# Attention and experts on one core: the value products dealt out by credit, their evictions placed anew

## The chip, the cores and the metric

The kernel runs on one core of a Trainium2 chip. The metric is device time in microseconds (us) of one execution. The five engines run side by side, each in the order of its own program, and wait for one another through semaphores: TensorE (PE, with its weight loads shown apart as PEld), VectorE (DVE), ScalarE (ACT), GpSimd (POOL) and SyncE (SP), which here issues most of the DMAs.

## The reference

Two stages. The first is attention over 8 batches of 8 heads, 576 positions, 64 channels, in which scores that lie more than tau below their row's maximum are dropped:

```python
scores = scale * np.matmul(q, k.transpose(0, 1, 3, 2))
thresh = np.max(scores, axis=-1, keepdims=True) - tau
scores = np.where(scores >= thresh, scores, -1000000000.0)
...
attn = np.exp(scores)
attn = attn / (np.sum(attn, axis=-1, keepdims=True) + 1e-09)
return np.matmul(attn, v).astype(np.float32)
```

The second gives each of the 4608 resulting rows of 512 to one of 8 experts, at most 576 rows each, in order of falling gate logits, and puts the rows through that expert's two matrices:

```python
logits = x @ w_gate
...
for e in range(E):
    mask = assigned == e
    h = np.maximum(x[mask] @ w1[e], 0.0)
    out[mask] = h @ w2[e]
```

## The kernel before

**Tiles and slots.** Two heads make a pair; four pairs make a batch, 32 pairs in all. The scores of a pair are cut into 9 tiles of 128 rows by 576 keys (the ninth holds the last 64 rows of both heads). The attention runs in slots of two tiles, 4.5 slots to a pair and 18 to a batch. The loop `for s_ in range(-2,NT//2+2)` (line 261) writes each engine's program slot by slot; slot numbers here are the values of `s_`. What stands earlier there stands earlier in the engine's queue. In slot s the tiles go through these steps:

- scores of tiles 2s+4 and 2s+5 by TensorE into `sc` (line 69). There are two such buffers, so the next slot's scores wait until VectorE has read these.
- first pass by VectorE (line 74): scale, row minimum, copy to `z`. This is the head of a slot as the trace is cut here. ScalarE takes the exponential (line 85), GpSimd adds tau to the threshold (line 75).
- second pass by VectorE (line 89), one slot later: drop what is under the threshold, and sum.
- transposes by TensorE into `tb` (line 98), two slots after the scores. There is one such buffer of two tiles, so they wait until ScalarE has evicted the slot before (lines 114, 116) into `pt`.
- in the slot after a pair's ninth tile, the leftover keys (64 of the 576) are transposed as well, ten small transposes ahead of the slot's other work (lines 118 and 122), and evicted into `pl` (lines 121, 127, 128). They use the same buffer `tb`. I call these leftover slots; each pair has one.

**Value products.** For a pair, the product with the values has two halves of 288 rows. Each half needs four units (line 139, two matmuls each, by 128 keys) and a last column (line 145, two matmuls, from the leftover keys), all summed in one bank `xo`. ScalarE evicts each half into `xt` (line 148).

**What orders them.** `queue` holds the units of all pairs that are ready, in order; `aux` holds the work of a finished batch: the swap of reciprocals (line 159), two halves of the gate logits (line 170), their transposes (lines 177 and 187), and for batches 0 and 1 five row units that turn `xt` back into rows (line 199; VectorE scales them in line 206). All of these, and the halves `xo`, share two banks. The parts of a slot that place them:

- `columns` takes 2 units, or 3 where the queue is longer than 10 entries. While a pair is not begun, it lets up to `GAP`=3 pieces of `aux` go first.
- `whole` takes the last columns of both halves at once (`pl_units`), when the pair's units are all done; else, while no pair is open, up to two pieces of `aux`.
- `flush` issues the evictions that the slot before has left over, at the start of the slot, ahead of the transposes' evictions in ScalarE's queue. Both halves of a pair are evicted there together.

A pair's `pt` and `pl` are allocated with its first transposes (line 106), which need the pair two before to be finished.

After the last slot the rows of batches 2 to 7 are made, beside the search for the first expert's rows, and then the experts' stage runs. It depends on the logits of the last batch; its code is the same in both kernels.

Of the kernel before, what the change touches and what calls it, by code (L numbers as in the profile page):

```python
# [16 lines left out]
PSUM = bass.MemoryType.PSUM  # L17
IOA = bass.IndirectOffsetOnAxis
S=576; D=64; HS=288; QK=3*HS+2*S
PPB=8; LTB=1; VTB=5; HOLD=1; GAP=3; NBO=2; XAC=(4,); NDEF=4; XTB=4; XTY=1.05; XT0=2.0; XRB=2  # L20


def attention(ctx, tc, qk, vl, tau, wgd, xrows, xts, Lg, nb_batches, ident, swap, R, after_first):
    nc=tc.nc
# [70 lines left out]
    PT={}; PL={}; TB={}  # L95
# [6 lines left out]
        return TB[k]  # L102
    def tr(t,first):
        p,i=divmod(t,9)
        if p not in PT:
            PT[p]=wk.tile([128,2,4,S],F32,name="pt"); PL[p]=wk.tile([128,S],F32,name="pl")
        tb=bank(t,first)
        pv=pview(t)
        o=64 if (i<8 and i%2) else 0
        for kb in range(4): turn(tb[:,:,kb],pv[:,o+kb*128:o+(kb+1)*128])  # L110
    def trev(t):
        p,i=divmod(t,9); tb=TB.pop(t)
        if i<8:
            A.activation(PT[p][:,i%2,:,(i//2)*128:(i//2+1)*128].rearrange("p k (r q) -> p r k q",r=2),tb,AF.Copy)  # L114
        else:
            A.activation(PT[p][:,:,:,512:576],tb,AF.Copy)
# [13 lines left out]

    have={}
    XT={}; XO={}
    def pv_unit(p,f,u):
        b,j=divmod(p,4)
        if b not in XT: XT[b]=wk.tile([128,4,S],F32,name="xt",bufs=XTB)
        if u==0: XO[p,f]=ps_v.tile([128,512],F32,name="xo")
        xo=XO[p,f]; q=slice(f*HS,(f+1)*HS); v=LD[p]["v"]
        for h in range(2):
            T.matmul(xo[64*h:64*h+64,:HS],v[:,u,64*h:64*h+64],PT[p][:,h,u,q],start=(u==0),stop=False,skip_group_check=True)  # L139
    def pl_units(p):  # L140
        b,j=divmod(p,4)
        for f in range(2):
            q=slice(f*HS,(f+1)*HS); xo=XO[p,f]
            for h in range(2):
                T.matmul(xo[64*h:64*h+64,:HS],LD[p]["v"][:,4,64*h:64*h+64],PL[p][:,q],start=False,stop=True,skip_group_check=True)
# [4 lines left out]

    RD={}
    def rd_calc(b):
        rd=wk.tile([128,4,9],F32,name="rd",bufs=XTB+NBO); RD[b]=rd
        V.tensor_scalar(rd,DEN[b],1e-9,None,op0=ALU.add)
        V.reciprocal(rd,rd)
    def rd_unit(b):
        rd=RD[b]
        ps=ps_v.tile([128,512],F32,name="xo")
        T.matmul(ps[:,:4],swap,rd[:,:,8],start=True,stop=True)
        rm=wk.tile([128,4,2],F32,name="rm",bufs=XTB+NBO); RD["m",b]=rm  # L160
        def ev():
            V.tensor_copy(rm[0:64,:,0],rd[0:64,:,8]); V.tensor_copy(rm[64:128,:,1],rd[64:128,:,8])
            V.tensor_copy(rm[0:64,:,1],ps[0:64,:4]); V.tensor_copy(rm[64:128,:,0],ps[64:128,:4])
        return ev
    LT={}
    def lg_unit(b,f):
        if f==0: LT[b]=wk.tile([128,S+D],F32,name="lt",bufs=LTB)
        ps=ps_v.tile([128,512],F32,name="xo")
        for j in range(4):
            T.matmul(ps[32*j:32*j+32,:HS],wg[:,j],XT[b][:,j,f*HS:(f+1)*HS],start=True,stop=True,tile_position=(0,32*j))  # L170
        def ev():
            A.activation(LT[b][:,f*HS:(f+1)*HS],ps[:,:HS],AF.Copy)
            if f==1: G.tensor_scalar(LT[b][:,S:],LT[b][:,S-D:S],1.0,0.0,op0=ALU.mult,op1=ALU.add)
        return ev
    def lgt_unit(b):
        ps=ps_v.tile([128,4,128],F32,name="xo")
        for c in range(4): T.transpose(ps[:,c],LT[b][:,c*128:(c+1)*128],ident)
        def ev():
            w=wk.tile([128,4,2,4,8],F32,name="lw",bufs=1)
            lv=ps.rearrange("p c (j r) -> p c j r",j=4)  # L180
            for h in range(2):
                V.tensor_tensor(w[:,:,h],lv[:,:,:,8*h:8*h+8],RD[b][:,:,h:8:2].rearrange("p j c -> p c j").unsqueeze(3).to_broadcast([128,4,4,8]),op=ALU.mult)
            V.tensor_reduce(Lg[:,4*b:4*b+4,:],w.rearrange("p c h j e -> p c e (h j)"),axis=AX.X,op=ALU.add)
        return ev
    def lgm_unit(b):
        ps=ps_v.tile([128,4,128],F32,name="xo")
        T.transpose(ps[:,0],LT[b][:,512:640],ident)
        r=slice(64*(b%2),64*(b%2)+64)
        def ev():
            w=wk.tile([128,4,2,8],F32,name="lwm",bufs=1)  # L190
            lv=ps[:,0].rearrange("p (j r) -> p j r",j=4)[:,:,:16].rearrange("p j (h e) -> p j h e",h=2)
            V.tensor_tensor(w[r],lv[r],RD["m",b][r].unsqueeze(3).to_broadcast([64,4,2,8]),op=ALU.mult)
            V.tensor_reduce(Lg[r,32+b//2,:],w[r].rearrange("p j h e -> p e (j h)"),axis=AX.X,op=ALU.add)
        return ev
    def xt_unit(b,c):
        ps=ps_v.tile([128,4,128],F32,name="xo")
        n=128 if c<4 else 64
        for j in range(4):
            T.transpose(ps[:n,j],XT[b][:,j,c*128:c*128+n],ident)
# [18 lines left out]
    def push_pair(p):  # L220
        b,j=divmod(p,4)
        for f in range(2):
            for u in range(4):
                need=(p,"t5" if f==0 else "t8")
                queue.append(("c",lambda need=need: have.get(need,1<<30)+HOLD<=st["slot"],lambda f=f,u=u: pv_unit(p,f,u)))
        if j==3: queue.append(("n",lambda: True,lambda: rd_calc(b)))
        queue.append(("f",lambda: have.get((p,"pl"),1<<30)+HOLD<=st["slot"],lambda: pl_units(p)))
        if (b,j)==(0,0): queue.append(("n",lambda: True,R.consts))
        if (b,j)==(nb_batches-1,2): queue.append(("n",lambda: True,lambda: (R.prep(0,28),R.compare(R.k("E1"),J,0,28))))
        if j==3:  # L230
            queue.append(("n",lambda: True,lambda: aux.extend([(0,lambda: rd_unit(b)),(0,lambda: lg_unit(b,0)),(0,lambda: lg_unit(b,1)),
                (1,lambda: lgt_unit(b)),(0,lambda: lgm_unit(b))])))
            rows=[lambda c=c: xt_unit(b,c) for c in range(5)]
            if nb_batches-NDEF-NBO<=b<nb_batches-NDEF:
                queue.append(("n",lambda: True,lambda: nc.sync.dma_start(xts[b],XT[b])))
                late2.extend(rows)
            elif b<nb_batches-NDEF: queue.append(("n",lambda: True,lambda: aux.extend([(0,x) for x in rows])))
            else: late.extend(rows)
# [3 lines left out]
    def plain():
        while queue and queue[0][0]=="n" and queue[0][1]() and not later: queue.pop(0)[2]()
    def columns(n):
        while n and queue and queue[0][0]=="c" and queue[0][1]():
            if not st["open"] and aux and st["aux"]<GAP and st["slot"]>=st["last"]+aux[0][0]: return
            queue.pop(0)[2](); st["open"]=True; n-=1
    def whole():
        while queue and queue[0][0]=="n" and queue[0][1]() and st["open"]: queue.pop(0)[2]()
        if st["open"]:  # L250
            if queue and queue[0][0]=="f" and queue[0][1]():
                later.append(queue.pop(0)[2]()); st["open"]=False; st["aux"]=0
            return
# [543 lines left out]
```

## Time and profile before

| | us |
|---|---|
| median of 3 runs | 1052.82 (1052.12 to 1054.36) |
| profiled execution, time | 1053.07 |
| profiled execution, span from first to last instruction | 1051.3 |
| head of the first slot (s = -2) | 5.39 |
| head of slot 23 | 86.02 |
| head of slot 59 | 215.50 |
| heads of slots 77, 95 and 113 (three batches on end) | 275.29, 335.34, 395.12 |
| head of the last slot (s = 141) | 489.42 |

A span runs from the first to the last instruction of the execution; the time of the run is a little longer. The attention fills the first half of the span. Shares of busy time over the span (PE 93%, DVE 74%, ACT 61%, POOL 32%) are means over both stages; what a change in the attention is worth is read from windows inside it.

In a time line a row gives the start, the length, the engine, line and operation, what is written and from what, the count, and in brackets the idle time before it and who ended it. Ends of matmuls are modelled; the distance from one start to the next is what a group takes of TensorE's time.

### The profile page before, as it was taken

Reading aid. Unit: us, or ns where it says so; the run is one execution under the profiler, and the core shown is the slowest. Engines: PE = TensorE matmul, PEld = TensorE weight load, DVE = VectorE, ACT = ScalarE, POOL = GpSimd, SP = SyncE. Lnnn points to the kernel's source line nnn. Section 1 sums busy time; section 2 is a strip of 40 time slices with the busy share of each in tenths; the row PEclk is TensorE's granted clock in tenths of the full one; section 3 lists DMA queues with packets and bytes.
Section 4 is the critical chain, followed back from the end, with each engine's and each line's share of the span. In section 5 each row is a group of like instructions: output and inputs, shape, how many; then the busy total and the mean of one; then the engine's idle time right before and its main releaser. Section 6 shows DMA issues by size and latency. Waiting matters only on the chain. (4 is left out here: it accounts for less than half of the span.)

```text
span 1051.3 us, 24035 instructions
## 1 busy us (share of the span) xinstructions
PE 977.3 (93%) x9104; PEld 715.4 (68%) x9104; DVE 777.3 (74%) x2085; ACT 640.4 (61%) x1221; POOL 331.3 (32%) x485
## 2 busy tenths in 40 slices
PE   6899999999999999999767999999999999999996
PEld 3555555555555555555457869889797988889895
DVE  6989988988989899898567767758586677744230
ACT  5888787888888888887454434435353534445340
POOL 2333443433333333333453535420303021132201
PEclk9999999999999999999877999999999999999998
DMA  5212331342422222111455061432424042363101
GB/s 220 105 60 100 119 110 48 131 154 102 150 104 68 92 105 105 55 53 50 163 187 169 12 198 48 149 108 91 156 91 161 17 151 106 103 234 126 51 9 42
DMA packets 35715, 113.03 MB, mean 108 GB/s; under 512 B 4368, under 2 KB 4752, under 8 KB 35088
## 3 DMA queue, kind: packets, MB, share of 16 engines
q1 hardware_dynamic: 28496, 89.47, 23.9%
q0 software_dynamic: 5888, 18.88, 5.7%
q10 hardware_dynamic: 1216, 3.15, 0.9%
q8 instruction: 72, 1.18, 0.5%
q14 instruction: 43, 0.35, 0.1%
HBM read 89.19 MB, written 21.23 MB: 105 GB/s over the span
## 5 line engine op out<-in xcount | busy, mean ns | idle before, releaser
L75 POOL TENSOR_SCALAR nb<-nb,taub 128x1 f32<-128x1 f32 x288 | 158.1, 550 | 302.8 <-DVE z L74 272.3
L74 DVE TENSOR_SCALAR_CACHE_REDUCE z<-sc 128x576 f32<-128x576 f32 x288 | 206.0, 751 | 49.4 <-PE sc L69 48.6
L85 ACT ACTIVATE pp<-z,nb 128x576 f32<-128x576 f32 x256 | 187.3, 772 | 35.9 <-DVE z L74 34.9
L89 DVE SCALAR_TENSOR_TENSOR pp<-z,nb,pp 128x576 f32<-128x576 f32 x256 | 199.9, 813 | 0.3
L664 PE MATMUL pf<-w2h,H 128*128 128x512 f32 x576 | 196.1, 402 | 1.1 <-DVE H L340 1.1
L69 PE MATMUL sc<-qk 64*128 64x288 f32 (+1 forms) x1280 | 183.4, 430 | 7.4 <-DMA qk<-qk_dram 6.1
L139 PE MATMUL xo<-pt,vt 128*64 128x288 f32 x1024 | 147.4, 416 | 4.4 <-DVE xr L206 2.8
L98 PEld LDWEIGHTS tb<-ident,pp 64*128 64x128 f32 x2304 | 85.8, 139 | 90.2 <-ACT pt L114 36.8
L114 ACT ACTIVATE pt<-tb 128x512 f32<-128x512 f32 x256 | 139.7, 592 | 6.7 <-PE tb L98 4.0
L98 PE MATMUL tb<-ident,pp 64*128 64x64 f32 x2304 | 108.8, 230 | 21.6 <-ACT pt L114 14.6
L664 PE MATMUL pf<-w2l,H 128*128 128x512 f32 x320 | 128.2, 401 | 0.0
L671 POOL DMA_INDIRECT out_dram<-y,idx x40 | 41.3, 1033 | 267.9 <-ACT y L667 163.1
L69 PEld LDWEIGHTS sc<-qk 64*128 64x128 f32 (+1 forms) x1280 | 93.3, 179 | 40.4 <-DVE z L74 9.2
L664 PEld LDWEIGHTS pf<-w2h,H 128*128 128x128 f32 x576 | 106.4, 189 | 20.0 <-DVE H L340 1.5
L644 PE MATMUL pf<-xh,w1h 128*128 128x288 f32 x512 | 113.3, 300 | 1.2 <-ACT xh L627 1.2
L644 PE MATMUL pf<-xh,w1l 128*128 128x288 f32 x512 | 113.7, 300 | 0.0
L644 PE MATMUL pf<-xl,w1h 128*128 128x288 f32 x512 | 113.0, 299 | 0.0
L139 PEld LDWEIGHTS xo<-pt,vt 128*64 128x64 f32 x1024 | 64.6, 136 | 67.1 <-issue 27.7
L650 ACT ACTIVATE hf<-pf 128x576 f32<-128x576 f32 x64 | 41.7, 651 | 105.4 <-PE pf L644 92.0
L667 ACT ACTIVATE y<-pf 128x512 f32<-128x512 f32 x40 | 23.9, 597 | 116.0 <-PE pf L664 99.4
L644 PEld LDWEIGHTS pf<-xh,w1h 128*128 128x128 f32 x512 | 82.9, 189 | 3.7 <-ACT xh L627 1.7
L644 PEld LDWEIGHTS pf<-xl,w1h 128*128 128x128 f32 x512 | 82.6, 189 | 0.2 <-DVE xl L340 0.2
(170 smaller groups left out, 1350.0 us busy)
## 6 DMA issues: line engine op xcount, KB each, us to landing
qk<-qk_dram SPq DMA_DIRECT2D x31, 1008.0 KB, 5.5
w2s<-w_dram SPq DMA_DIRECT2D x32, 512.0 KB, 6.0
w1s<-w_dram SPq DMA_DIRECT2D x28, 512.0 KB, 5.6
vt<-vl_dram SPq DMA_DIRECT2D x32, 320.0 KB, 5.8
xrows<-pp SPq DMA_DIRECT2D x24, 256.0 KB, 2.0
xts<-xt SPq DMA_DIRECT2D x2, 1152.0 KB, 5.2
pt<-xts SPq DMA_DIRECT2D x2, 1152.0 KB
xrows<-xr SPq DMA_DIRECT2D x8, 256.0 KB, 2.1
```

The costliest lines, as they stand in the source:

```text
L69: T.matmul(sc[o,f,:HS], kd["q",h][r,c], kd[k,h][r,:],start=True,stop=True)
L74: V.tensor_scalar(z,SC.pop(t)[:,:,:HS],-0.125,None,op0=ALU.mult,op1=ALU.min,accum_out=nb[:,0:1])
L75: G.tensor_scalar(nb[:,1:2],nb[:,0:1],taub[:,0:1],None,op0=ALU.add)
L85: A.activation(pview(t),ZB[t].rearrange("p a b -> p (a b)"),AF.Exp,bias=NBI[t][:,0:1],scale=-1.0)
L89: V.scalar_tensor_tensor(pv,ZB.pop(t).rearrange("p a b -> p (a b)"),NBI[t][:,1:2],pv,op0=ALU.is_le,op1=ALU.mult,accum_out=den_of(p)[:,p%4, ...
L98: g=slice(64*r,64*r+64); T.transpose(o[:,r],x[g],ident[g,g])
L114: A.activation(PT[p][:,i%2,:,(i//2)*128:(i//2+1)*128].rearrange("p k (r q) -> p r k q",r=2),tb,AF.Copy)
L139: T.matmul(xo[64*h:64*h+64,:HS],v[:,u,64*h:64*h+64],PT[p][:,h,u,q],start=(u==0),stop=False,skip_group_check=True)
L644: T.matmul(ps[:,h,:HS],s[w][:,k,f*128:(f+1)*128],s[x][:,k,h*HS:(h+1)*HS], start=(k==0 and j==0),stop=(k==3 and j==2))
L650: A.activation(hf,ps[:,:,:HS],AF.Relu)
L664: T.matmul(ps[:,0,:],H[:,f,c:c+128],s[w][:,f],start=(f==0 and j==0),stop=e)
L671: G.indirect_dma_start(out=out,out_offset=IOA(ap=s["idx"][:n,t:t+1],axis=0),in_=y[:n],in_offset=None)
```

## The change

The units are dealt out by a credit: each slot adds `RATE`=2.4, up to `CAPV`=3.3, and each unit and each half's last column takes 1. The last column follows its own half's four units (`pl_unit`), and each half is evicted when it is done. A half is only begun when the bank of two halves before is free (`free_v`). Work of `aux` is placed only when no half is open, so behind a last column; `columns` stops there for it.

In slots in which the ninth tile is evicted (the leftover slots), `flush` moves behind the transposes' evictions. `pt` and `pl` are allocated at the first eviction instead of the first transposes.

```diff
-PPB=8; LTB=1; VTB=5; HOLD=1; GAP=3; NBO=2; XAC=(4,); NDEF=4; XTB=4; XTY=1.05; XT0=2.0; XRB=2
+PPB=8; LTB=1; VTB=5; HOLD=1; CAPV=3.3; RATE=(2.4,2.4); NBO=2; XAC=(4,); NDEF=4; XTB=4; XTY=1.05; XT0=2.0; XRB=2
...
     def trev(t):
         p,i=divmod(t,9); tb=TB.pop(t)
+        if i==0: PT[p]=wk.tile([128,2,4,S],F32,name="pt"); PL[p]=wk.tile([128,S],F32,name="pl")
...
+    banks=[]; VB={}
+    def bank_v(sh):
+        t=ps_v.tile(sh,F32,name="xo"); banks.append([False]); VB[id(t)]=banks[-1]
+        return t
+    def free_v(): return len(banks)<2 or banks[-2][0]
...
-    def pl_units(p):
+    def pl_unit(p,f):
         b,j=divmod(p,4)
-        for f in range(2):
-            q=slice(f*HS,(f+1)*HS); xo=XO[p,f]
-            for h in range(2):
-                T.matmul(xo[64*h:64*h+64,:HS],LD[p]["v"][:,4,64*h:64*h+64],PL[p][:,q],start=False,stop=True,skip_group_check=True)
-        have[p,"pv"]=1
-        def ev():
-            for f in range(2): A.activation(XT[b][:,j,f*HS:(f+1)*HS],XO.pop((p,f))[:,:HS],AF.Copy)
-        return ev
+        q=slice(f*HS,(f+1)*HS); xo=XO.pop((p,f))
+        for h in range(2):
+            T.matmul(xo[64*h:64*h+64,:HS],LD[p]["v"][:,4,64*h:64*h+64],PL[p][:,q],start=False,stop=True,skip_group_check=True)
+        if f==1: have[p,"pv"]=1
+        return VB[id(xo)],lambda: A.activation(XT[b][:,j,q],xo[:,:HS],AF.Copy)
...
+        for f in range(2):
+            for u in range(4): queue.append(("c",when("t5" if f==0 else "t8"),u==0,lambda f=f,u=u: pv_unit(p,f,u)))
+            if (f,j)==(0,3): queue.append(("n",when("t8"),False,lambda: rd_calc(b)))
+            queue.append(("c",when("pl"),False,lambda f=f: pl_unit(p,f)))
...
+    def columns():
+        while queue and queue[0][1]():
+            if queue[0][0]=="c":
+                if st["credit"]<1 or (queue[0][2] and not free_v()): return
+                st["credit"]-=1
+            c,_,_,g=queue.pop(0); r=g()
+            if c=="c" and r:
+                later.append(r)
+                if aux: return
     def whole():
...
         n=0
-        while n<2 and aux and st["slot"]>=st["last"]+aux[0][0]:
-            r=aux.pop(0)[1](); n+=1; st["aux"]+=1; st["last"]=st["slot"]
+        while n<2 and aux and not XO and free_v() and st["slot"]>=st["last"]+aux[0][0]:
+            r=aux.pop(0)[1](); n+=1; st["last"]=st["slot"]
...
-        flush(); plain()
+
+        if not any(t%9==8 for t in ev_): flush()
         for t in ev_:
-            p,i=divmod(t,9); trev(t); have[p,f"t{i}"]=s_
+            p,i=divmod(t,9)
+            while i==0 and p>1 and (p-2,"pv") not in have: st["credit"]=9; columns(); flush()
+            trev(t); have[p,f"t{i}"]=s_
+        flush()
...
-        columns(3 if len(queue)>10 else 2)
-        if any(t%9==0 and t>=18 for t in tr_):
-            while (max(tr_)//9-2,"pv") not in have: columns(9); whole(); flush(); plain()
-        else: whole()
+        st["credit"]=min(st["credit"]+RATE[bool(aux)],CAPV)
+        columns(); whole()
```

What this does to TensorE's program in a steady batch (slots 95 to 112 in both kernels), beside the scores and the sixteen transposes that every slot has. "Left" is the leftover block, "v" a value unit, "c" one half's last column, "swap" the swap of reciprocals, "g" one half of the logits, "t" their transposes; "(6)" marks the slots with a ninth tile of scores, which have six matmuls for scores in place of four. VectorE's work from the swap, the logits' transposes and the row units stands between a slot's second pass and the next head; the reciprocals (lines 154 and 155) stand in the 17th slot before, in the 15th after.

| slot of the batch | before | after |
|---|---|---|
| 1 | left, swap, g | left, 2v |
| 2 (6) | g | c, swap |
| 3 | 2v | 3v |
| 4 | 3v | v, c, g |
| 5 | left, 3v, 2c | left, 3v |
| 6 | 5t | v, c, g |
| 7 (6) | 2v | 2v |
| 8 | 3v | 2v, c, 4t |
| 9 | 3v, 2c | 2v |
| 10 | left, 2v | left, 2v |
| 11 (6) | 2v | c, 1t |
| 12 | 2v | 3v |
| 13 | 2v, 2c | v, c |
| 14 | left, 3v | left, 3v |
| 15 | 2v | v, c |
| 16 (6) | 2v | 2v |
| 17 | v, 2c | 2v, c |
| 18 | none | 2v |

In slots 23 to 58 the five row units of batches 0 and 1 ("x") are placed too. Before, they stand two, two and one to a slot (slots 29, 32, 33 and 47, 50, 51). After, one to a slot, and the logits of batch 1 move back. These slots then differ from the table:

| slot | after | slot | after |
|---|---|---|---|
| 35 | v, c, x | 48 | 2v, c, g |
| 37 | v, c, x | 51 | c, g |
| 39 | 2v, c, x | 53 | v, c, 4t |
| 42 | c, x | 55 | v, c, 1t |
| 44 | v, c, x | 57 | 2v, c, x |
| 46 | v, c, swap | | |

The other four row units of batch 1 stand in slots 60, 62, 64 and 66.

TensorE's rows at slot 117, the fifth of a batch, and the one behind it. `sc` are scores, `tb` transposes, `xo<-pt,vt` value units (two rows each), `xo<-pl,vt` last columns, `xo<-xt,wg` and `xo<-ident,lt` the logits. Before:

```order
L69 MATMUL sc<-qk 128x288 x4
L98 MATMUL tb<-ident,pp 128x64 x8
L98 MATMUL tb<-ident,pm 128x64 x2
L139 MATMUL xo<-pt,vt 64x288 x6
L145 MATMUL xo<-pl,vt 64x288 x4
L98 MATMUL tb<-ident,pp 128x64 x16
L69 MATMUL sc<-qk 128x288 x4
L177 MATMUL xo<-ident,lt 128x128 x4
L187 MATMUL xo<-ident,lt 128x128
L98 MATMUL tb<-ident,pp 128x64 x16
```

And after:

```order
L69 MATMUL sc<-qk 128x288 x4
L98 MATMUL tb<-ident,pp 128x64 x8
L98 MATMUL tb<-ident,pm 128x64 x2
L144 MATMUL xo<-pt,vt 64x288 x6
L98 MATMUL tb<-ident,pp 128x64 x16
L69 MATMUL sc<-qk 128x288 x4
L144 MATMUL xo<-pt,vt 64x288 x2
L149 MATMUL xo<-pl,vt 64x288 x2
L172 MATMUL xo<-xt,wg 32x288 x4
L98 MATMUL tb<-ident,pp 128x64 x16
```

The four matmuls of the last columns have left the leftover slot; the slot behind it now holds a value unit, one half's last column and half of the logits.

ScalarE's rows at two leftover slots. `pt<-tb` evicts transposes, `xt<-xo` a half of the values' product, `pl<-tb` the leftover keys, `pp<-z,nb` is the exponential. Before (slot 104's kind, the tenth of a batch, with both halves of the slot before in front):

```order
L148 ACTIVATE xt<-xo 128x288 x2
L116 ACTIVATE pt<-tb 128x8x64
L114 ACTIVATE pt<-tb 128x2x4x64
L121 ACTIVATE pl<-tb 128x2x4x64
L127 ACTIVATE pl<-tb 64x64
L128 ACTIVATE pl<-tb 64x64
```

After (slot 108's kind, the fourteenth, which follows a last column):

```order
L113 ACTIVATE pt<-tb 128x2x4x64
L115 ACTIVATE pt<-tb 128x8x64
L151 ACTIVATE xt<-xo 128x288
L120 ACTIVATE pl<-tb 128x2x4x64
L126 ACTIVATE pl<-tb 64x64
L127 ACTIVATE pl<-tb 64x64
```

The eviction of a half now stands behind those of the transposes and ahead of that of the leftover keys, and it is one where there were two.

More of the change, by code (lines that the diff above doesn't have):

```diff
@@ L104, in tr @@
         p,i=divmod(t,9)
-        if p not in PT:
-            PT[p]=wk.tile([128,2,4,S],F32,name="pt"); PL[p]=wk.tile([128,S],F32,name="pl")
         tb=bank(t,first)
@@ L135, in pv_unit @@
         if b not in XT: XT[b]=wk.tile([128,4,S],F32,name="xt",bufs=XTB)
-        if u==0: XO[p,f]=ps_v.tile([128,512],F32,name="xo")
+        if u==0: XO[p,f]=bank_v([128,512])
         xo=XO[p,f]; q=slice(f*HS,(f+1)*HS); v=LD[p]["v"]
@@ L157, in rd_unit @@
         rd=RD[b]
-        ps=ps_v.tile([128,512],F32,name="xo")
+        ps=bank_v([128,512])
         T.matmul(ps[:,:4],swap,rd[:,:,8],start=True,stop=True)
@@ L167, in lg_unit @@
         if f==0: LT[b]=wk.tile([128,S+D],F32,name="lt",bufs=LTB)
-        ps=ps_v.tile([128,512],F32,name="xo")
+        ps=bank_v([128,512])
         for j in range(4):
@@ L175, in lgt_unit @@
     def lgt_unit(b):
-        ps=ps_v.tile([128,4,128],F32,name="xo")
+        ps=bank_v([128,4,128])
         for c in range(4): T.transpose(ps[:,c],LT[b][:,c*128:(c+1)*128],ident)
@@ L185, in lgm_unit @@
     def lgm_unit(b):
-        ps=ps_v.tile([128,4,128],F32,name="xo")
+        ps=bank_v([128,4,128])
         T.transpose(ps[:,0],LT[b][:,512:640],ident)
@@ L195, in xt_unit @@
     def xt_unit(b,c):
-        ps=ps_v.tile([128,4,128],F32,name="xo")
+        ps=bank_v([128,4,128])
         n=128 if c<4 else 64
@@ L214, in xt_unit, with when @@
         return ev
-    queue=[]; aux=[]; later=[]; late=[]; late2=[]; st={"open":False,"aux":0,"last":-9,"slot":0}
+    queue=[]; aux=[]; later=[]; late=[]; late2=[]; st={"last":-9,"slot":0,"credit":0.0}
     def push_pair(p):
         b,j=divmod(p,4)
+        def when(n): return lambda: have.get((p,n),1<<30)+HOLD<=st["slot"]
         for f in range(2):
[L223 to L238, printed above, removed]
@@ new lines, in push_pair @@
+            for u in range(4): queue.append(("c",when("t5" if f==0 else "t8"),u==0,lambda f=f,u=u: pv_unit(p,f,u)))
+            if (f,j)==(0,3): queue.append(("n",when("t8"),False,lambda: rd_calc(b)))
+            queue.append(("c",when("pl"),False,lambda f=f: pl_unit(p,f)))
+        if (b,j)==(0,0): queue.append(("n",lambda: True,False,R.consts))
+        if (b,j)==(nb_batches-1,2): queue.append(("n",lambda: not aux,False,lambda: (R.prep(0,28),R.compare(R.k("E1"),J,0,28))))
+        if j==3: queue.append(("n",lambda: not later,False,lambda: finish(b)))
@@ L239, in flush, with finish @@
+    def finish(b):
+        aux.extend([(0,lambda: rd_unit(b)),(0,lambda: lg_unit(b,0)),(0,lambda: lg_unit(b,1)),(1,lambda: lgt_unit(b)),(0,lambda: lgm_unit(b))])
+        rows=[lambda c=c: xt_unit(b,c) for c in range(5)]
+        if nb_batches-NDEF-NBO<=b<nb_batches-NDEF:
+            nc.sync.dma_start(xts[b],XT[b]); late2.extend(rows)
+        elif b<nb_batches-NDEF: aux.extend([(0,x) for x in rows])
+        else: late.extend(rows)
     def flush():
-        for g in later: g()
+        for k,g in later: g(); k[0]=True
@@ L241, in flush @@
         later.clear()
[L242 to L247, printed above, removed]
-    def whole():
[L249 to L253, printed above, removed]
-        n=0
-        while n<2 and aux and st["slot"]>=st["last"]+aux[0][0]:
-            r=aux.pop(0)[1](); n+=1; st["aux"]+=1; st["last"]=st["slot"]
-            if callable(r): later.append(r)
+    def columns():
[7 more added lines that the diff above has]
+                if aux: return
@@ L258, in attention @@
+    def whole():
+        n=0
+        while n<2 and aux and not XO and free_v() and st["slot"]>=st["last"]+aux[0][0]:
+            r=aux.pop(0)[1](); n+=1; st["last"]=st["slot"]
+            later.append((banks[-1],r))
     load(0);
@@ L286, in attention @@
     while queue or aux or later:
-        st["slot"]+=1; flush(); plain(); columns(9); whole()
+        st["slot"]+=1; st["credit"]=9; flush(); columns(); whole()
     for k in range(0,NBO,2):
```

## The prediction

> **What bounds the kernel now.** I read the page first, for its span, then the list of waits over the attention, then windows cut at batch borders, and last the time lines of VectorE and TensorE inside one batch.
>
> ```profile
> span 1051.3 us, 24035 instructions
> ```
> ```profile
> DVE z L74 <- PE sc L69: 48.6, 43, 3.8
> ```
> The second row is from the waits of the first 530 us. VectorE's first pass (line 74) is the head of every slot, and in 43 slots it stood still for scores, 48.6 us in all.
>
> A slot is two tiles of scores; 18 slots are one batch. These windows run from the head of one slot to the head of a later one (columns: length; busy us and count of PE, PEld, DVE, ACT, POOL; clock; DMA share; GB/s).
>
> ```profile
> 275.29:335.34 60.05, 57.55 (x671) 33.69 (x671) 54.66 (x158) 51.18 (x95) 19.83 (x41) 1.00 0.33 118
> 86.02:215.50 129.48, 120.48 (x1382) 71.80 (x1382) 114.80 (x321) 103.49 (x189) 49.62 (x82) 1.00 0.28 102
> ```
> A steady batch is 60.05 us with VectorE busy for 54.66: at most 5.4 us of a batch can be gained by removing waits alone. The second window is 36 slots in which ten units of row output are made as well.
>
> How short can a slot be? VectorE's time line, two successive heads without a wait, and two with one:
>
> ```profile
> 281.80 0.75 DVE L74 TENSOR_SCALAR_CACHE_REDUCE z<-sc 128x576 f32<-128x576 f32 x1
> 284.64 0.75 DVE L74 TENSOR_SCALAR_CACHE_REDUCE z<-sc 128x576 f32<-128x576 f32 x1
> ...
> 287.52 0.76 DVE L74 TENSOR_SCALAR_CACHE_REDUCE z<-sc 128x576 f32<-128x576 f32 x1
> 292.44 0.76 DVE L74 TENSOR_SCALAR_CACHE_REDUCE z<-sc 128x576 f32<-128x576 f32 x1 [2.00 <-PE sc L69]
> ```
> The first is 2.84 us, VectorE's own pace. The second is 4.92 with 2.00 of waiting. TensorE in that slot and the next:
>
> ```profile
> 286.77 1.19 PE L69 MATMUL sc<-qk 64*128 64x288 f32 x8
> 288.11 0.46 PE L98 MATMUL tb<-ident,pp 64*128 64x64 f32 x8 [0.15 <-ACT pt L116]
> ...
> 288.56 1.68 PE L139 MATMUL xo<-pt,vt 128*64 128x288 f32 x12
> 290.07 1.14 PE L145 MATMUL xo<-pl,vt 128*64 128x288 f32 x8
> 291.14 0.71 PE L98 MATMUL tb<-ident,pp 64*128 64x64 f32 x16
> 291.69 1.19 PE L69 MATMUL sc<-qk 64*128 64x288 f32 x8
> 292.81 0.66 PE L177 MATMUL xo<-ident,lt 128*128 128x128 f32 x4
> 293.30 0.27 PE L187 MATMUL xo<-ident,lt 128*128 128x128 f32 x1
> 293.50 0.71 PE L98 MATMUL tb<-ident,pp 64*128 64x64 f32 x16
> ```
> From start to start: scores 1.12, leftover block 0.45 after a wait of 0.15, twelve value records 1.51, the last columns of both halves 1.07, transposes 0.55. TensorE is simply full here: from scores to scores 4.92. The next slot has almost nothing on it. So the wait comes from **lumps**, and dealing the value units evenly attacks it.
>
> **The change, part by part.** No product is added or removed. The trace counts a value matmul twice and a transpose once, so the prices are: a slot's scores and transposes 1.67; one value unit 1.51/3 = 0.50 (I use 0.51); one half's last column 1.07/2 = 0.535; leftover block 0.60 with its wait; four transposes of logits 0.49, a single one 0.20. The others:
>
> ```profile
> 277.82 1.35 PE L69 MATMUL sc<-qk 64*128 64x288 f32 x12
> 279.10 0.69 PE L170 MATMUL xo<-xt,wg 128*32 128x288 f32 x8
> ...
> 504.07 1.18 PE L170 MATMUL xo<-xt,wg 128*32 128x288 f32 x16 [0.54 <-DVE rm L163]
> 505.28 0.92 PE L177 MATMUL xo<-ident,lt 128*128 128x128 f32 x4
> ...
> 106.66 1.35 PE L199 MATMUL xo<-ident,xt 128*128 128x128 f32 x8 [0.37 <-DVE lw L182]
> 107.94 0.71 PE L98 MATMUL tb<-ident,pp 64*128 64x64 f32 x16
> ```
> Twelve score records take 1.28 (0.16 over eight), one half of the logits 1.21/2 = 0.60, a row unit 1.28/2 = 0.64. VectorE's side work, which lengthens its slot beyond 2.84:
>
> ```profile
> 295.29 0.48 DVE L182 TENSOR_TENSOR lw<-xo,rd 128x128 f32<-128x128 f32 x2
> ...
> 296.45 0.23 DVE L192 TENSOR_TENSOR lwm<-xo,rm 64x64 f32<-64x64 f32 x1
> ...
> 297.01 0.76 DVE L74 TENSOR_SCALAR_CACHE_REDUCE z<-sc 128x576 f32<-128x576 f32 x1
> ```
> ```profile
> L206 DVE TENSOR_TENSOR xr<-xo,rd 128x512 f32<-128x512 f32 x8 | 5.1, 681 | 0.0
> L155 DVE RECIPROCAL rd<-rd 128x36 f32<-128x36 f32 x8 | 3.0, 378 | 0.3
> L162 DVE COPY rm<-rd 64x4 f32<-64x4 f32 x16 | 2.6, 161 | 0.2
> L163 DVE COPY rm<-xo 64x4 f32<-64x4 f32 x16 | 2.6, 160 | 6.2 <-PE xo L159 6.0
> L154 DVE TENSOR_SCALAR rd<-den 128x36 f32<-128x36 f32 x8 | 1.6, 206 | 0.0
> ```
> Logits 1.16 and 0.56, a row unit 0.68, reciprocals 0.59, four copies 0.64. A leftover slot also has a chain through ScalarE (evict, transpose the leftovers, evict, transpose) that no dealing shortens. Measured, with eight value records and with twelve:
>
> ```profile
> 306.35 0.76 DVE L74 TENSOR_SCALAR_CACHE_REDUCE z<-sc 128x576 f32<-128x576 f32 x1 [0.63 <-PE sc L69]
> 309.82 0.76 DVE L74 TENSOR_SCALAR_CACHE_REDUCE z<-sc 128x576 f32<-128x576 f32 x1 [0.55 <-PE sc L69]
> ...
> 319.32 0.76 DVE L74 TENSOR_SCALAR_CACHE_REDUCE z<-sc 128x576 f32<-128x576 f32 x1 [0.79 <-PE sc L69]
> 323.28 0.76 DVE L74 TENSOR_SCALAR_CACHE_REDUCE z<-sc 128x576 f32<-128x576 f32 x1 [1.04 <-PE sc L69]
> ```
> They are 3.47 and 3.96; both kinds remain, two of each in a batch.
>
> Now I give each of a batch's 18 slots the larger of TensorE's sum and VectorE's. **Before:** 3.48, 2.84, 2.84, 3.20, 4.87, 4.56, 2.85, 3.20, 4.27, 3.47, 2.85, 2.84, 3.76, 3.96, 2.84, 2.85, 3.43, 2.84, together 60.95. **After**, in the new order (the work of each slot is in the first table of the section on the change): 3.47, 3.48, 3.20, 3.32, 3.96, 3.32, 2.85, 4.00, 2.84, 3.47, 3.40, 3.20, 2.84, 3.96, 3.43, 2.85, 3.23, 2.84, together 59.66. The rule gives 0.90 too much for before (60.05 measured), because TensorE gets ahead in a slot that VectorE sets and spends that lead in the next. After the change there are three such places: the 3.48 leaves a lead of 0.80 (TensorE's own sum there is 2.68), which takes 0.80 of the 0.36 and 0.48 that the next two slots lie over 2.84; the 3.40 saves the slot behind it 0.36, and the 3.43 the 3.23 two behind it 0.39: 1.55 together.
>
> **What it adds.** Evictions of a half now stand alone at the head of ScalarE's queue in light slots too, ahead of the transposes' evictions. The trace shows one such slot, with the logits' eviction of the same size:
>
> ```profile
> 278.71 0.41 ACT L172 ACTIVATE lt<-xo 128x288 f32<-128x288 f32 x1
> 279.02 1.08 ACT L114 ACTIVATE pt<-tb 128x512 f32<-128x512 f32 x2
> ...
> 280.15 0.71 PE L98 MATMUL tb<-ident,pp 64*128 64x64 f32 x16 [0.36 <-ACT pt L114]
> ...
> 278.84 0.76 DVE L74 TENSOR_SCALAR_CACHE_REDUCE z<-sc 128x576 f32<-128x576 f32 x1
> ```
> TensorE waits 0.36 for it, behind it the next scores, but the slot from 278.84 to 281.80 is only 2.96, so 0.12 over the pace. Its price lies between nothing and 0.41; I take 0.12, the row itself, for three light slots a batch: 0.36. In leftover slots the same eviction now stands behind the two transposes' evictions, beside the leftovers' transposes (0.45 of TensorE), which hide it; without that cover it would cost up to 0.41 there.
>
> So a steady batch becomes 59.66 - 1.55 + 0.36 = 58.47, a gain of 1.58. From slot 59 there are 84 slots, 4.67 batches: 7.4 us.
>
> Slots 23 to 58, where rows are made: the new order differs from two steady batches (119.32) in the slots that the second table of the section on the change lists: 35, 37 and 39 by +0.68, +0.68, +0.64 (a row unit on VectorE or TensorE), 42, 44 and 46 by +0.04, +0.20, +0.16, 48 and 51 by -0.17, -0.43, 53, 55 and 57 by +1.16, +0.56, +0.64. That is +4.16, so 123.5; less 3.1 of lead, plus 0.7 of evictions: 121.1 against 129.48. Four of the ten row units have moved behind slot 58, where they cost 4 x 0.68 = 2.7. Gain: 8.4 - 2.7 = 5.7. For the 23 slots before, whose loads and constants stay, an estimate of 0.5. At the end the first half's eviction goes beside the second half's matmuls: 0.4. All of it lies on the path, as every slot's head waits for the one before, and the experts' stage starts after the attention's last logits.
>
> Sum: 7.4 + 5.7 + 0.5 + 0.4 = 14.0. The profiled execution took 1053.07 us, 1.77 more than its span: 1053.07 - 14.0 = 1039.1. The median, 1052.82, is 0.25 lower: **1039**.
>
> [...]
>
> **The rivals.**
> - *Lead isn't carried.* If ScalarE's chain keeps TensorE from getting ahead, a steady batch is 59.66 + 0.36 = 60.02, no gain there; slots 23 to 58 still give 129.48 - 123.5 - 0.7 - 2.7 = 2.6, the rest 0.9: 3.5 gained, 1049. For it: the wait of 0.36 above. Against it: the old order shows 0.90 of carrying.
> - *All waits go.* A batch falls near VectorE's 54.66; even half-way (57.4) is 2.7 a batch, and 129.48 - 114.80 = 14.7 is open in slots 23 to 58. Half of 5.4 over 4.67 batches is 12.6, half of 14.7 is 7.3, with 0.9: 21, so 1032; two thirds of it give 1026. Against it: four leftover slots a batch keep their chain, 2.5 us over the pace.
> - *Slower.* Each of the 64 half-evictions pushes its transposes, and so the next scores, by its full 0.41: 26.2 us against 14.0 + 2.5 of gain, so 1053.1 + 9.7 = 1063. It decides once an eviction costs 0.26. Against it: the one row shows 0.12.
> - *It doesn't do what it says.* The rows in the section on the change show one to three value units in nearly every slot, where before they lay in lumps of up to five (with last columns) beside empty slots; this has no share.
>
> **How the numbers follow.** Forecast (1033 to 1045): 0.55. Little carried (1045 to 1050): 0.16. Most waits gone (1026 to 1033): 0.15. Beyond that: 0.02. Slower, or level within 0.2% (2.1 us, about what a measurement of this kernel can tell from no change): 0.07 and 0.05. The range takes in the first three, 0.86 of the chance: 1026 to 1050. Faster by over 0.2%: 0.55 + 0.16 + 0.15 + 0.02 = 0.88; within: 0.05; slower: 0.07.
>
> **What would show it.** VectorE's wait for scores falls from 48.6 to about 35, with no wait near 2.00 in a steady batch; such a batch takes about 58.5; leftover slots still 3.5 to 4.0; slots of 36 with rows near 121. It would be wrong if light slots with an eviction come out at 3.2 or more, if leftover slots change, or if the experts' stage takes another time than before.

## The result and the profile after

The changed kernel took **1035.63 us** (median of 4 runs, 1034.96 to 1037.0) against 1052.47 (4 runs, 1051.77 to 1054.36): a ratio of 0.984, interval 0.9828 to 0.9853. The forecast was 1039, in a range of 1026 to 1050. The profiled execution took 1035.21 us.

The page's span, and from the waits of the first 515 us the one for scores (columns: us in total, times, longest):

```profile
span 1033.4 us, 24027 instructions
```
```profile
DVE z L74 <- PE sc L69: 32.5, 46, 4.0
```
The wait was 48.6 us before. It has lost 16.1 us, about as much as the kernel has gained. The number of waits is about the same (43 before, 46 now): they have become shorter, not fewer.

The windows between heads of the same slots (slots 23 to 58, 95 to 112, 113 to 130, and from the last slot's head to the end):

```profile
84.33:204.63 120.30, 119.03 (x1370) 69.08 (x1366) 112.47 (x319) 102.74 (x189) 42.30 (x82) 1.00 0.28 98
323.32:381.54 58.22, 57.60 (x675) 33.32 (x671) 54.30 (x158) 51.07 (x95) 21.80 (x41) 1.00 0.27 95
381.54:440.12 58.58, 57.59 (x675) 33.29 (x671) 54.57 (x158) 51.12 (x95) 19.86 (x41) 1.00 0.27 95
473.59:1033.40 559.81, 517.83 (x3850) 444.93 (x3850) 340.60 (x840) 236.91 (x488) 159.02 (x152) 0.97 0.34 114
```
The second and third rows are two steady batches, now 58.22 and 58.58 us. The same slots took 59.78 and 60.04 before, so each batch has lost about 1.5 us, with the same busy time on every engine to within 0.4 us (VectorE 54.37 and 54.66 before, 54.30 and 54.57 now). Slots 23 to 58 have gone from 129.48 to 120.30. No work left the kernel; idle time did.

The heads of slots 99, 100, 101, 106 and 107 on VectorE, and TensorE's rows in two stretches of that batch, slot 99 to 101 and slot 105 to 106:

```profile
336.21 0.76 DVE L74 TENSOR_SCALAR_CACHE_REDUCE z<-sc 128x576 f32<-128x576 f32 x1
340.16 0.76 DVE L74 TENSOR_SCALAR_CACHE_REDUCE z<-sc 128x576 f32<-128x576 f32 x1 [1.03 <-PE sc L69]
343.70 0.76 DVE L74 TENSOR_SCALAR_CACHE_REDUCE z<-sc 128x576 f32<-128x576 f32 x1 [0.61 <-PE sc L69]
...
360.07 0.73 DVE L74 TENSOR_SCALAR_CACHE_REDUCE z<-sc 128x576 f32<-128x576 f32 x1
362.90 0.74 DVE L74 TENSOR_SCALAR_CACHE_REDUCE z<-sc 128x576 f32<-128x576 f32 x1
```
```profile
336.80 0.46 PE L98 MATMUL tb<-ident,pp 64*128 64x64 f32 x8 [0.15 <-ACT pt L115]
...
339.41 1.19 PE L69 MATMUL sc<-qk 64*128 64x288 f32 x8
340.52 0.71 PE L144 MATMUL xo<-pt,vt 128*64 128x288 f32 x4
341.06 0.66 PE L149 MATMUL xo<-pl,vt 128*64 128x288 f32 x4
341.65 0.69 PE L172 MATMUL xo<-xt,wg 128*32 128x288 f32 x8
...
358.76 1.19 PE L69 MATMUL sc<-qk 64*128 64x288 f32 x8
359.88 1.68 PE L144 MATMUL xo<-pt,vt 128*64 128x288 f32 x12
361.48 0.71 PE L98 MATMUL tb<-ident,pp 64*128 64x64 f32 x16
362.03 1.19 PE L69 MATMUL sc<-qk 64*128 64x288 f32 x8
```
Slot 99 is the leftover slot that took 4.92 us with both last columns in it. It now takes 3.95 (336.21 to 340.16), and its successor 3.54 instead of 4.32 (4.56 in the batch that the prediction shows), with one unit, one last column and half of the logits there. Slot 106 shows how a lead is spent. It holds three units, and TensorE needs 3.27 us from scores to scores (358.76 to 362.03). Yet VectorE's heads are only 2.83 apart (360.07 to 362.90) and no wait is shown: the scores had been started 1.31 us ahead of the first of these heads, and 0.87 ahead of the second. TensorE gave up 0.44 us of its lead, and nobody waited.

### The profile page after: what moved, and what is told of

It is laid out like the page before. It is cut to its first block, busy times and chain, and to the rows that moved or that the text cites. A ratio compares the mean times of both kernels' runs of the same rounds, so it can differ in the third digit from the quotient of the medians.

```text
span 1033.4 us, 24027 instructions
## 1 busy us (share of the span) xinstructions
PE 975.2 (94%) x9104; PEld 709.5 (69%) x9104; DVE 777.4 (75%) x2085; ACT 640.0 (62%) x1221; POOL 323.1 (31%) x485
## 5 line engine op out<-in xcount | busy, mean ns | idle before, releaser
L75 POOL TENSOR_SCALAR nb<-nb,taub 128x1 f32<-128x1 f32 x288 | 146.8, 510 | 296.6 <-DVE z L74 256.1
L74 DVE TENSOR_SCALAR_CACHE_REDUCE z<-sc 128x576 f32<-128x576 f32 x288 | 206.0, 752 | 34.0 <-PE sc L69 32.5
L69 PE MATMUL sc<-qk 64*128 64x288 f32 (+1 forms) x1280 | 181.3, 428 | 6.0 <-DMA qk<-qk_dram 5.7
L144 PE MATMUL xo<-pt,vt 128*64 128x288 f32 x1024 | 151.9, 418 | 0.7 <-ACT xt L151 0.7
L98 PEld LDWEIGHTS tb<-ident,pp 64*128 64x128 f32 x2304 | 85.7, 139 | 72.7 <-ACT pt L113 16.8
L144 PEld LDWEIGHTS xo<-pt,vt 128*64 128x64 f32 x1024 | 62.5, 136 | 63.6 <-issue 26.5
```

What stands on the lines that cost most here:

```text
L69: T.matmul(sc[o,f,:HS], kd["q",h][r,c], kd[k,h][r,:],start=True,stop=True)
L74: V.tensor_scalar(z,SC.pop(t)[:,:,:HS],-0.125,None,op0=ALU.mult,op1=ALU.min,accum_out=nb[:,0:1])
L75: G.tensor_scalar(nb[:,1:2],nb[:,0:1],taub[:,0:1],None,op0=ALU.add)
L98: g=slice(64*r,64*r+64); T.transpose(o[:,r],x[g],ident[g,g])
```

## The experiments

**The order undone, the dealing kept** (e1). In leftover slots the half's eviction goes to the front of ScalarE's queue again:

```diff
-        if not any(t%9==8 for t in ev_): flush()
+        flush()
```


> The changed kernel with the one step undone that moves the leftover evictions in leftover slots: the halves' evictions stand in front of the transposes' evictions again, as in all other slots. If that order matters, the two leftover slots of a batch that follow a last column lose 0.41 us each, and the one with half of the logits 0.41 more: up to 1.2 us a batch, 5 to 9 us in all, so about 1042. If the eviction runs beside TensorE's transposes anyway, nothing: 1035 to 1036.5.

1040.24 us (1039.32 to 1041.32), ratio to before 0.9864 (0.9848 to 0.988). Slot by slot against the changed kernel, apart from the first slot, only nine leftover slots differ by more than 0.08: 18, 27, 72, 90, 99, 108, 117, 126 and 135, each by 0.29 to 0.35, together 2.9 us. (The first slot was 0.74 longer in this execution; TensorE's waits for loads of `qk` are 6.3 us in it and 5.7 in the changed kernel's.) That is less than the 5 to 9 us expected: each slot lost a little less than 0.41, and only nine of the 32 leftover slots lost more than 0.08. The runs agree with the 2.9: the kernel before took 1054.39 beside these runs, so the gain here is 14.2 us, 2.7 less than the changed kernel's 16.8. ScalarE at slot 99 (its head is at 338.12 here), and TensorE's leftover block behind it:

```profile
337.33 0.39 ACT L151 ACTIVATE xt<-xo 128x288 f32<-128x288 f32 x1
337.62 0.40 ACT L174 ACTIVATE lt<-xo 128x288 f32<-128x288 f32 x1
337.91 0.60 ACT L113 ACTIVATE pt<-tb 128x512 f32<-128x512 f32 x1
338.39 0.61 ACT L115 ACTIVATE pt<-tb 128x512 f32<-128x512 f32 x1
```
```profile
339.05 0.46 PE L98 MATMUL tb<-ident,pp 64*128 64x64 f32 x8 [0.49 <-ACT pt L115]
```
And ScalarE in the changed kernel at the same slot, and at slot 106 (the last two rows), a light slot in which the half's eviction stays in front:

```profile
335.66 0.60 ACT L113 ACTIVATE pt<-tb 128x512 f32<-128x512 f32 x1 [0.15 <-PE tb L98]
336.15 0.59 ACT L115 ACTIVATE pt<-tb 128x512 f32<-128x512 f32 x1
336.63 0.42 ACT L151 ACTIVATE xt<-xo 128x288 f32<-128x288 f32 x1
...
359.19 0.41 ACT L151 ACTIVATE xt<-xo 128x288 f32<-128x288 f32 x1
359.48 1.09 ACT L113 ACTIVATE pt<-tb 128x512 f32<-128x512 f32 x2
```
In front, the two evictions keep `tb` occupied longer: TensorE waits 0.49 us for the buffer instead of the 0.15 quoted above, and the slot becomes 4.29 instead of 3.95. The difference in the wait, 0.34, is the difference in the slot. So the new order gives 2.9 us, and the dealing gives the larger part: with the dealing alone the last slot's head stands at 477.15, against 489.42 before and 473.59 after.

**The order alone, put into the kernel before** (e2).

```diff
-        flush(); plain()
+        late_ev=any(t%9==8 for t in ev_)
+        if not late_ev: flush(); plain()
...
+        if late_ev: flush(); plain()
```


> The kernel before with that one step alone (in leftover slots the halves' evictions come behind the transposes'); lumps as before. If the gain is from the even dealing, this is the kernel before within 1 us, 1052 to 1053. If the order of the evictions brings the gain, it is below 1045.

1054.18 us against 1054.39 beside it: ratio 1.0 (0.9991 to 1.0009). The last slot's head stands at 489.49. The reason is on ScalarE at slot 90, a leftover slot behind two last columns; first the kernel before, then this one:

```profile
317.77 0.78 ACT L148 ACTIVATE xt<-xo 128x288 f32<-128x288 f32 x2
318.77 0.60 ACT L114 ACTIVATE pt<-tb 128x512 f32<-128x512 f32 x1 [0.23 <-PE tb L98]
```
```profile
318.80 0.60 ACT L114 ACTIVATE pt<-tb 128x512 f32<-128x512 f32 x1 [0.91 <-PE tb L98]
319.30 0.59 ACT L116 ACTIVATE pt<-tb 128x512 f32<-128x512 f32 x1
```
With the lumps, TensorE is so late with the transposes that ScalarE has done both evictions in front and still waits 0.23 us. Moving them behind turns that into an idle 0.91, and the transposes' eviction starts no earlier: at 318.80, where it was 318.77 (this execution runs 0.03 later throughout). The order is worth something only once TensorE is no longer late: its 2.9 us are made possible by the dealing.

**Value units thinned out in both kernels** (e3 after, e4 before). Three of four value units of each half are left out, so the output lacks those products, and the lumps are gone:

```diff
+        if u: return
```


> The changed kernel with three of each half's four value units left out (their products are missing from the output; order, evictions and all else stay). 192 units of 0.51 us, 98 us of TensorE's work, are gone. If TensorE's load in the full slots is what is left of the waits, slots without leftovers go to VectorE's own pace, 2.84 us plus its side work, and only the 32 leftover slots keep about 3.4: VectorE's wait for scores falls from 32.5 to about 18 us, the time to about 1021. If ScalarE's evictions in light slots hold the pace, slots with an eviction stay above 2.95 and the wait stays above 25.

> The kernel before with the same three units of each half left out. If lumps of TensorE's work are the whole difference of the two kernels, this one and the changed kernel with the same cut now end within 4 us of each other. If the placing of the evictions or of the finished batch's work made the difference, it stays 10 us or more behind.

e3: 1031.34 us in a single run, wait for scores 29.3. e4: 1026.28 and 28.8. The numbers expected for both were missed. e3 was to take about 1021; part of the reason is in the last section. e4 was to end within 4 us of e3 and ended 5.06 ahead of it, not 10 or more behind as the rival had it: 3.4 of that is in the experts' stage (561.8 in e3, 558.4 in e4), whose code is the same, and why it differs stays open. The head of the last slot, where the attention ends, in e3, then in e4:

```profile
467.78 0.76 DVE L74 TENSOR_SCALAR_CACHE_REDUCE z<-sc 128x576 f32<-128x576 f32 x1 [0.74 <-PE sc L69]
```
```profile
466.14 0.76 DVE L74 TENSOR_SCALAR_CACHE_REDUCE z<-sc 128x576 f32<-128x576 f32 x1 [1.91 <-PE sc L69]
```
The whole kernels reach the same head at 489.42 (before) and 473.59 (after), 15.8 us apart. Without three quarters of the units the distance is 1.6 us, and it is the kernel before that leads. On the way it changes sign several times and is never over 3.0 (0.02 at slot 93, 2.8 at slot 81). So the 15.8 us hang on how the units are placed, and on what their placing makes of the order on ScalarE; to within about 3 us, nothing else in the change gives or costs anything once they are thinned.

**Lumps put back, all else kept** (e5). Each slot gets credit for nine units, so units are issued as soon as they are ready; halves are still evicted one by one, and the order on ScalarE stays:

```diff
-CAPV=3.3; RATE=(2.4,2.4);
+CAPV=9.0; RATE=(9.0,9.0);
```


> The changed kernel with a credit of 9 a slot and a cap of 9: each half's four units and last column are issued as soon as they are ready, all else as changed. It has the changed kernel's split evictions and their order, but lumps of up to eight value matmuls and two last columns beside empty slots. The sum over a batch, slot by slot the larger of TensorE's and VectorE's work, is 66.2 us less about 2 of lead, against 58.2 to 58.6 measured for the even dealing. If the lumps price the slots, this takes 1070 to 1085. If the split evictions brought the gain, it stays below 1045.

1075.14 us in a single run, within what was expected: 22.9 us over the kernel before beside it (1052.21). The wait for scores, three heads (slots 99 to 101) and TensorE between scores:

```profile
DVE z L74 <- PE sc L69: 69.2, 63, 4.0
```
```profile
361.83 0.75 DVE L74 TENSOR_SCALAR_CACHE_REDUCE z<-sc 128x576 f32<-128x576 f32 x1
...
366.12 0.76 DVE L74 TENSOR_SCALAR_CACHE_REDUCE z<-sc 128x576 f32<-128x576 f32 x1 [1.38 <-PE sc L69]
...
370.97 0.76 DVE L74 TENSOR_SCALAR_CACHE_REDUCE z<-sc 128x576 f32<-128x576 f32 x1 [1.93 <-PE sc L69]
```
```profile
365.37 1.19 PE L69 MATMUL sc<-qk 64*128 64x288 f32 x8
366.49 0.71 PE L149 MATMUL xo<-pl,vt 128*64 128x288 f32 x4
367.02 2.11 PE L144 MATMUL xo<-pt,vt 128*64 128x288 f32 x16
368.96 0.66 PE L149 MATMUL xo<-pl,vt 128*64 128x288 f32 x4
...
370.19 1.40 PE L69 MATMUL sc<-qk 64*64 64x288 f32 x12
```
Four units and two last columns make a slot of 4.85 us again (366.12 to 370.97). The same products, the same evictions and the same order on ScalarE cost 39.5 us more (1075.14 against 1035.63) by the credit's numbers alone; 37.0 of it is in the attention, where the head of the last slot comes at 510.60 instead of 473.59.

**Each half's eviction done twice** (e6), to price an eviction and to test the slower rival:

```diff
+        def ev2():
+            for n in range(2): A.activation(XT[b][:,j,q],xo[:,:HS],AF.Copy)
...
-        return VB[id(xo)],lambda: A.activation(XT[b][:,j,q],xo[:,:HS],AF.Copy)
+        return VB[id(xo)],ev2
```


> The changed kernel with each half's eviction done twice by ScalarE (64 more of 0.41 us, same values). If ScalarE has room between the exponentials and the transposes' evictions, as the forecast's 0.12 a slot says, it takes 1036 to 1043. If an eviction holds the pace with its full length, as the slower rival says, 26 us more: about 1060.

1042.15 us (1041.77 to 1042.3), ratio 0.9899 (0.9883 to 0.9916). The last slot's head comes at 476.93, 3.3 us later than after, for 64 more evictions of 0.41 us: 0.05 each. In the batch of slots 95 to 112 only four slots grow by 0.1 or more: 98 (+0.16), 99 (+0.29), 106 (+0.12) and 108 (+0.11). ScalarE has room for most of it. The time, though, has lost 6.8 us of the gain over the kernel before beside it (1052.21). The rest of that is in the experts' stage, 563.6 us in this profile, the longest of all; why is open.

**At most two units in a leftover slot** (e7). The changed kernel's leftover slots 99, 108 and so on hold three units and take 3.8 to 3.95; those with two take 3.4. This version keeps the third unit's credit for the next slot:

```diff
-        st["credit"]=min(st["credit"]+RATE[bool(aux)],CAPV)
-        columns(); whole()
+        lo=any(t%9==8 for t in ev_); keep=0.0
+        st["credit"]=min(st["credit"]+RATE[bool(aux)],CAPV+(1.0 if lo else 0.0))
+        if lo and st["credit"]>2: keep=st["credit"]-2; st["credit"]=2.0
+        columns(); whole(); st["credit"]+=keep
```


> The changed kernel with at most two units in a leftover slot; what it keeps back goes to the slot behind. Slots 5 and 14 of a batch hold two value units in place of three, slots 6 and 15 two in place of one. If a leftover slot's time is its chain through ScalarE (3.4) and TensorE's third unit comes on top, slots 5 and 14 fall from 3.95 and 3.80 to about 3.45; slot 15 has VectorE's reciprocals beside it and takes the unit for nothing, slot 6 grows by 0.3: about 0.5 a batch, so 1031 to 1033. If the third unit fitted into the chain, no change: 1035 to 1036.

1037.18 us (1036.98 to 1037.37), ratio 0.9854 (0.9837 to 0.987): a miss, no gain over the changed kernel. Heads of slots 99 to 101, and TensorE's scores in the second of these slots and the next:

```profile
336.73 0.76 DVE L74 TENSOR_SCALAR_CACHE_REDUCE z<-sc 128x576 f32<-128x576 f32 x1
...
340.23 0.76 DVE L74 TENSOR_SCALAR_CACHE_REDUCE z<-sc 128x576 f32<-128x576 f32 x1 [0.58 <-PE sc L69]
...
344.25 0.76 DVE L74 TENSOR_SCALAR_CACHE_REDUCE z<-sc 128x576 f32<-128x576 f32 x1 [1.10 <-PE sc L69]
```
```profile
339.47 1.19 PE L69 MATMUL sc<-qk 64*128 64x288 f32 x8
...
343.46 1.40 PE L69 MATMUL sc<-qk 64*64 64x288 f32 x12
```
Slot 99 fell from 3.95 to 3.50, and slot 100 rose from 3.54 to 4.02: the pair takes 7.52 instead of 7.49. Between those scores TensorE has no wait (two units, one last column, half of the logits, transposes: 3.99 us from scores to scores). The unit's time has moved to a slot that TensorE already set. No version that was run with all its products beats the changed kernel.

**Both kernels profiled again** (e8 and e10 the changed kernel, e9 the kernel before, unedited). The experts' stage, whose code is the same, was 2.1 us shorter in the first profile of the changed kernel (559.81 against 561.88, from the last slot's head to the end). Does the change cause that?

> The changed kernel itself, profiled once more, to see how long the experts' stage (head of slot 141 to the end of the span) is in another execution of the same program. Theory: that stage's length belongs to the execution and not to the change, so it may come out anywhere from 559.5 to 563.5 us (the seven profiles so far lie from 559.8 to 563.6), while the head of slot 141 stays within 0.6 us of 473.59. Rival: the change shortens the stage by 2.1 us, so it comes out again at 559.3 to 560.3.

> The kernel before, profiled once more, for the same question. Theory: the experts' stage anywhere from 559.5 to 563.5 us, head of slot 141 within 0.6 us of 489.42. Rival (the change shortens the stage): again 561.4 to 562.4, above every profile of the changed kernel.

> The changed kernel a third time, same question: by the theory the three profiles of one program differ among themselves by as much as before and after do, 1 us or more; by the rival they agree within 0.5 us at about 559.8.

The stage in e8, then in e9:

```profile
473.65:1035.80 562.15, 523.47 (x3850) 449.83 (x3850) 339.27 (x840) 236.81 (x488) 158.19 (x152) 0.96 0.33 113
```
```profile
489.80:1052.00 562.20, 522.97 (x3857) 449.25 (x3857) 340.06 (x838) 237.12 (x488) 157.41 (x152) 0.96 0.33 113
```
562.15 and 562.20, and in e10 562.25. Two of three profiles of the changed kernel have a stage as long as the kernel before; so the change does not shorten it, and the first profile had a quick one (its clock there was 0.97 against 0.96). The attention, by contrast, repeats closely: the last slot's head came at 473.59, 473.65 and 473.55 after, at 489.42 and 489.80 before. The gain of the attention is therefore 489.61 - 473.60 = **16.0 us**, and the medians' 16.8 lies within a microsecond of it.

## Why the prediction held, point by point

The mechanism was right: TensorE was full in a few slots and light in others, and dealing out the units evenly shortened the full ones. e5 puts the lumps back and loses 37.0 us in the attention; e3 and e4 take three quarters of the units away and bring the kernels within 3 us of each other all along it. The 1039 was 3.4 us too high. The terms account for 2.0 of it; the rest lies between executions (the median before is 0.35 lower than the one that the forecast started from, and the experts' stage varies). By its terms, in us:

| term | forecast | measured |
|---|---|---|
| first slots, to the head of slot 23 | 0.5 | 1.9 (mean lengths 80.77 before, 78.86 after) |
| slots 23 to 58, without the row units moved behind them | 8.4 | 9.18 (129.48 to 120.30) |
| from slot 59 to the last head, with those row units | 7.4 - 2.7 = 4.7 | 4.96 (273.92 to 268.96) |
| the end of the attention | 0.4 | 0.0 |
| sum | 14.0 | 16.0 |

- *First slots.* This term was the one most off. It was only an estimate, on the ground that loads and constants stay. 0.6 of the 1.9 is the very first slot (4.49 on the mean before, 3.93 after), where loads still arrive (in the first profiles TensorE waits 2.08 us for `qk` there before, 1.53 after); it takes 3.75 to 4.61 over the profiles of both kernels and their variants, 4.56 in e1, so this part is luck. From the second slot's head to that of slot 23 it is 76.28 before and 74.92 after: 1.4. There slots 12 and 16 were 3.76 each, with two units and both last columns, the kind of lump worked out for the batches; after, they take 2.84. They alone give 1.85, and the slots around them take 0.5 back.
- *Steady batch.* The forecast 58.47 lies between the 58.22 and the 58.58 measured. The slot rule (the larger of TensorE's sum and VectorE's) gave 59.66, with 1.55 taken off for lead and 0.36 put on for evictions. Measured slots 95 to 112 against that rule's list: -0.05, +0.08, -0.24, -0.37, -0.01, +0.22, +0.12, -0.11, -0.01, -0.08, -0.12, -0.37, -0.01, -0.16, -0.08, -0.07, -0.19, 0.00, together -1.45, and 59.66 - 1.45 = 58.21. The three places where lead was to be spent show: slots 3 and 4 of the batch (-0.61; 0.80 forecast), slot 12 (-0.37; 0.36), slot 17 (-0.19; 0.39): 1.17 in place of 1.55. This lead came out 0.38 too small and the 0.36 for evictions should have been near nothing (next point), so two errors of opposite sign nearly cancel, and that the batch came out as forecast is in part luck.
- *Eviction in light slots, 0.12 each.* Too high, and misread. The 0.12 was taken from slot 78 (278.84 to 281.80, 2.96 us). But slot 83 of the kernel before takes 2.96 too (297.01 to 299.97), and no half's and no logits' eviction stands on ScalarE there. In both, VectorE's second pass starts 0.11 to 0.12 us later behind the first than it does in slots of 2.84; so the row does not price an eviction. In slot 106 of the changed kernel the half's eviction (359.19) stands ahead of the transposes' (359.48), and the slot stays at 2.83; e6 prices an extra eviction at 0.05 on the mean.
- *Order in leftover slots, up to 0.41 without the cover.* Right in size where it counts: 0.29 to 0.35 in nine slots (e1). It was not foreseen that the order would be worth nothing with the lumps (e2).
- *The end.* The last half's eviction was to come 0.4 sooner. From the last slot's head to the first matmul of the logits it took 14.65 before and 14.63 after: nothing gained. The forecast took the first half's eviction off the path, but it was not on it. TensorE's wait ahead of the logits in the changed kernel:

```profile
488.22 1.18 PE L172 MATMUL xo<-xt,wg 128*32 128x288 f32 x16 [0.53 <-DVE rm L165]
```
The logits wait for VectorE's copies behind the swap of reciprocals, as in the kernel before (0.54, line 163, at 504.07), and these end after the evictions (at 488.08 against 487.83 in the changed kernel).
- *What would show it.* The wait for scores fell to 32.5 (about 35 forecast). In the batch of slots 95 to 112 it is 3.5 us in 5 waits, the longest 1.0, where the longest was 2.00. Leftover slots take 3.4 to 3.95.

Of the rivals, *the lead isn't carried* fell: slot 106 above, and 58.22 against its 60.02. *Slower* fell: its deciding price was 0.26 for an eviction, and e6 measured 0.05 in the attention (0.11 if all of the 6.8 us lost is counted). *It doesn't do what it says* fell with e5. *All waits go* did not come about: a batch keeps 3.9 us over VectorE's 54.30 (its half-way mark was 57.4), and e7 shows part of what holds it: TensorE, without a gap, in the slot next to the leftover slot.

## What to carry to other kernels

Where two engines take turns in slots and each is nearly full on average, add up each engine's starts slot by slot, not over the window: here the loss sat in the slots where TensorE was over VectorE's pace (4.92 us against 2.84), and dealing movable work by credit, with the evictions placed anew, recovered 16.0 us of it; what is left over is a chain or a slot that is full anyway (leftover slots of 3.4 to 3.95). An order on a third engine's queue can be worth nothing before such a change and something after it (here nothing in e2 and 2.9 us in e1), so try it again then. Apply the slot count to the start-up slots too (two of them gave 1.85 us here), and profile unchanged stages more than once before their difference is put down to a change (559.81 to 562.25 us in three profiles of one kernel).

## What the runs showed that was not expected

With work taken away from TensorE, its granted clock came out lower: over the whole execution 0.954 in e3 and 0.969 in e4, against 0.982 in the changed kernel and 0.980 in the kernel before. e3 was expected at about 1021 us and took 1031.34. Its windows of 4 us around 380 us (PEclk is the column before the DMA share), and TensorE there:

```profile
372.00:376.00 4.00, 2.52 (x38) 1.57 (x34) 4.00 (x13) 3.45 (x7) 1.49 (x3) 1.00 0.00 0
376.00:380.00 4.00, 2.98 (x36) 1.40 (x33) 3.02 (x9) 3.75 (x8) 1.26 (x3) 0.77 0.00 0
380.00:384.00 4.00, 4.00 (x30) 2.54 (x26) 3.03 (x11) 2.51 (x5) 0.69 (x1) 0.50 0.76 267
```
```profile
375.61 0.47 PE L98 MATMUL tb<-ident,pp 64*128 64x64 f32 x8 [0.79 <-ACT pt L113]
...
377.17 0.72 PE L98 MATMUL tb<-ident,pp 64*128 64x64 f32 x16 [1.02 <-ACT pl L127]
377.72 2.05 PE L69 MATMUL sc<-qk 64*128 64x288 f32 x12
...
382.29 2.24 PE L69 MATMUL sc<-qk 64*128 64x288 f32 x8
```
Behind two waits of 0.79 and 1.02 us the clock is 0.50 in the third window, and eight score records take 2.24 us instead of 1.19. From 350 to 400 us the mean is 0.89 in e3, 0.97 in e4, and 1.00 in the changed kernel: the thinned kernels lose part of what the thinning saves. In the changed kernel's attention nothing of this shows: its windows, quoted above, have 1.00.

Neither a single wait's length nor the idle share by itself tells when the clock falls. In the kernel before, TensorE waits 1.33 us in one piece ahead of 111.08, longer than either wait above, and from 86.02 to 215.50 its clock is 1.00. In e4 TensorE is busy for 2.44 of the 4 us from 372 and for 2.98 of those from 384, as little as in e3's first two windows (2.52 and 2.98), and the clock is 1.00 in all five windows of 4 us from 372 to 392.

Two places with slow scores in e3 differ in what stands ahead of them. From 374.82, the modelled end of the scores before, to 377.72 TensorE has only transposes and waits, 2.90 us. Eight score records at 361.78 take 2.24 us too, and there a value unit (359.77) stands between a wait of 1.02 and one of 0.45. What lowers the clock is not shown.

The experts' stage is of nearly 562 us and came out from 559.8 to 563.6 over the ten profiles of kernels with all products, all with the same code for it, while the head of the last slot came within 0.1 us in three profiles of the changed kernel (473.55 to 473.65) and within 0.4 in two of the kernel before (489.42 and 489.80). In e6 the four runs lie within 0.6 us of each other, so its long stage seems to have come four times, and not to be chance of one execution; what sets the stage's length is not shown.
